# Splitting the K and V loads over two issuing queues, and moving half of the output projection forward, in a grouped-query attention kernel that reads a cache

## The chip, the cores and the metric

The kernel runs on one core of a Trainium2 chip. The metric is the device time of one execution in microseconds (us). Each execution has a state: fast, slow (over 1.5% above the fastest of the same kernel), or unknown when a kernel ran only once.

Engines: PE is the tensor engine (PEld is its weight load, which overlaps the matmuls), ACT is ScalarE, DVE is VectorE, POOL is GpSimd, SP is SyncE. "SPq" and "ACTq" are the DMA-issuing instructions of SyncE and ScalarE. A "unit" is one batch with one pair of key/value heads; there are 32, and each needs one K load and one V load of 1 MB.

## The reference, cut to what matters

```python
# B, Sq, D = 8, 4, 512;  Hq, Hkv, Sk, Dh = 32, 8, 2048, 128;  bfloat16
q = (x @ wq) split into 32 heads of 128
k, v = k_cache, v_cache repeated for the 4 query heads of each kv head
scores = einsum("bhqd,bhkd->bhqk", q, k) * Dh ** -0.5
o = einsum("bhqk,bhkd->bhqd", softmax(scores), v)
return o.transpose(0, 2, 1, 3).reshape(B, Sq, Hq * Dh) @ wo
```

wq and wo are 4 MB each, the two caches 32 MB each: 72 MB are read for very little arithmetic.

## The kernel before: the parts that matter

All loads are issued by SyncE, one K and then one V, up to seven units ahead. Each unit is worked on in two halves ("steps"). The tensor engine transposes K, multiplies it with the queries, sums the denominators and multiplies the probabilities with V. ScalarE does the exponentials and one of the four copies of transposed K in each unit.

```python
def load(u):                                  # K, then V, on the sync queue
    ks[u] = kpool.tile([128, C, Dh], BF16, tag="k_sb", name="k_sb")
    nc.sync.dma_start(ks[u][:, :, :], k_cache[...])
    vs[u] = vpool.tile([128, C, Dh], BF16, tag="v_sb", name="v_sb")
    nc.sync.dma_start(vs[u][:, :, :], v_cache[...])
# ... (cut)
nc.sync.dma_start(wq_sb[:, :, :], wq...)
for u in range(PRE):                          # PRE = 7
    load(u)
# ... (cut: query projection)
for step in range(-2, NH):                    # NH = 64 half-units
    if step + 2 < NH:
        transpose_part(step + 2, 0)           # PE: 8 transposes (kp); then a copy (kt)
    if 0 <= step + 1 < NH:
        scores(step + 1)                      # PE: 16 matmuls (s_ps); ACT: 2 exponentials (probs)
    if step + 2 < NH:
        transpose_part(step + 2, 1)           # in odd half-units ACT makes the copy (kt)
    if step >= 0:
        values(step)                          # PE: denominators (l_ps), 16 matmuls with V (o_ps)
        if step % 2 == 1:
            u = step // 2 + PRE
            if u < NU:
                load(u)
            elif u == NU:
                for h0, n in WO_PIECES:       # six pieces of wo, after the last V
                    load_wo(h0, n)
for h in range(Hq):                           # whole projection at the end, 32 matmuls (out_ps)
    nc.tensor.matmul(out_ps, lhsT=oT_all[h], rhs=wo_sb[h], ...)
```

A landing semaphore is the counter that tells of a load's arrival. The traces show eight of them, given to the loads in turn. A load is issued only when the load that used its semaphore before has landed: K4 shares the one of K0, which landed at 16.10 us, and was issued at 16.11. When such a wait is next in an engine's instruction stream, the engine does nothing else until it ends (8.48 us of ScalarE, shown below).

The softmax here doesn't subtract the row's maximum and nothing guards it: scores larger than these inputs give would overflow.

## Time and profile before

| | before |
|---|---|
| time, median of 3 runs | 195.59 us (195.52 to 196.03) |
| span of the profiled run | 193.9 us |
| a K or V load lands every | 2.48 us (unit: 4.97 us) |
| last K, last V, last wo piece land | 175.7, 178.2, 189.6 us |
| attention ends (last o_ps matmul) | 183.7 us |
| projection ends | 190.8 us |

These are lines of the page of the profile of the kernel before. In the first four, the span is cut in 40 equal slices; a digit is the busy share, or the granted clock, in tenths, and GB/s is what the DMA engines moved. The next two are the chain of work that ended last, by engine and by line. The last is a group of instructions: count, busy time, mean ns of one, then the idle time before them and what ended it.

```profile
PE   1019698887788868988877878598887878877893
PEclk9999789999999996999999999889999999996999
DMA  6989999999999999999999999999999999999960
GB/s 223 433 382 429 414 419 428 411 422 419 411 429 407 416 424 416 421 419 414 422 416 419 421 414 422 421 416 421 417 414 419 414 421 426 411 394 320 328 208 7
...
DMA 88%; PE 7%; SPq 2%; ACT 1%; issue 0%; DVE 0%; ACTq 0%
DMA k_sb<-in_k_cache_dram 88%; PE out_ps L223 4%; PE kp L134 2%; SPq L79 1%; SPq L84 1%; PE s_ps L150 1%; ACT kt L137 1%; PE l_ps L169 0%; PE o_ps L189 0%; DVE out_sb L230 0%; ACTq L257 0%; SPq L70 0%; SPq L69 0%; ACT probs L156 0%; ACTq L156 0%
...
L134 PE MATMUL kp<-ident,k_sb 128*128 128x128 bf16 x1024 | 83.2, 228 | 29.2 <-DMA k_sb<-in_k_cache_dram 29.0
```

The DMA engines are full from about 5 us to the end, and the chain consists of K loads. In the middle the tensor engine is eight tenths busy. Its one large wait, 29.0 us, is for K; the transposes of a unit start 0.05 us after its K lands, in nearly every unit.

### The profile page before, as it was taken

What the parts mean: (1) busy time and instruction counts of PE and PEld (TensorE: products, weight loads), DVE (VectorE), ACT (ScalarE), POOL (GpSimd) and SP (SyncE); (2) the same over time, 40 slices, a digit from 0 to 9 for tenths busy, and PEclk for the clock granted to TensorE, in tenths of its full rate; (3) what the DMA queues carried; (4) which work ended last, traced back from release to release, by engine and by line L of the source; (5) the groups of instructions that cost most, each with busy time, mean ns of one, the idle gap of its engine ahead of it and who ended that gap; (6) DMA issues with size and microseconds to landing.
All of it is one profiled execution on the core that took longest, in us unless ns stands there. A gap on an engine that the chain in (4) does not pass through costs nothing.

```text
span 193.9 us, 7655 instructions
## 1 busy us (share of the span) xinstructions
PE 146.2 (75%) x3492; PEld 137.8 (71%) x3492; DVE 95.4 (49%) x201; ACT 83.5 (43%) x165; POOL 0.7 (0%) x6
## 2 busy tenths in 40 slices
PE   1019698887788868988877878598887878877893
PEld 0019598777787768987777777498877777777741
DVE  4002366556555554665566665265555556663401
ACT  2003455444445551654444544355455555551500
POOL 1000000000000000000000000000000000000000
PEclk9999789999999996999999999889999999996999
DMA  6989999999999999999999999999999999999960
GB/s 223 433 382 429 414 419 428 411 422 419 411 429 407 416 424 416 421 419 414 422 416 419 421 414 422 421 416 421 417 414 419 414 421 426 411 394 320 328 208 7
DMA packets 13680, 76.05 MB, mean 392 GB/s; under 512 B 1168, under 2 KB 5328, under 8 KB 5328
## 3 DMA queue, kind: packets, MB, share of 16 engines
q1 hardware_dynamic: 13648, 75.57, 95.7%
q8 instruction: 27, 0.44, 0.9%
q14 instruction: 5, 0.04, 0.1%
HBM read 75.53 MB, written 0.03 MB: 390 GB/s over the span
## 4 chain that ended last, share of the span: by engine, by line
DMA 88%; PE 7%; SPq 2%; ACT 1%; issue 0%; DVE 0%; ACTq 0%
DMA k_sb<-in_k_cache_dram 88%; PE out_ps L223 4%; PE kp L134 2%; SPq L79 1%; SPq L84 1%; PE s_ps L150 1%; ACT kt L137 1%; PE l_ps L169 0%; PE o_ps L189 0%; DVE out_sb L230 0%; ACTq L257 0%; SPq L70 0%; SPq L69 0%; ACT probs L156 0%; ACTq L156 0%
## 5 line engine op out<-in xcount | busy, mean ns | idle before, releaser
L134 PE MATMUL kp<-ident,k_sb 128*128 128x128 bf16 x1024 | 83.2, 228 | 29.2 <-DMA k_sb<-in_k_cache_dram 29.0
L139 DVE COPY kt<-kp 128x1024 bf16<-128x1024 bf16 x96 | 66.0, 691 | 61.8 <-PE kp L134 50.8
L134 PEld LDWEIGHTS <-k_sb 128*128 128x128 bf16 x1024 | 62.6, 102 | 32.2 <-DMA k_sb<-in_k_cache_dram 31.9
L156 ACT ACTIVATE probs<-s_ps 64x256 bf16<-64x256 f32 x128 | 48.3, 378 | 83.7 <-PE s_ps L150 82.1
L150 PE MATMUL s_ps<-qT_all,kt 128*128 128x32 bf16 x1024 | 37.1, 177 | 1.0 <-ACT kt L137 0.5
L189 PE MATMUL o_ps<-probs,v_sb 128*128 128x32 bf16 x1024 | 36.1, 177 | 0.5 <-issue 0.5
L150 PEld LDWEIGHTS <-kt 128*128 128x128 bf16 x1024 | 33.4, 97 | 1.6 <-DVE kt L139 0.7
L189 PEld LDWEIGHTS <-v_sb 128*128 128x128 bf16 x1024 | 32.9, 97 | 0.6 <-issue 0.6
L137 ACT COPY kt<-kp 128x1024 bf16<-128x1024 bf16 x32 | 32.4, 1012 | 0.8
L169 PE MATMUL l_ps<-probs,ones 128*128 128x128 bf16 x256 | 20.0, 219 | 0.7 <-issue 0.4
L177 DVE TENSOR_REDUCE l_sb<-l_ps 128x32 f32<-128x128 f32 x32 | 9.3, 291 | 21.9 <-PE l_ps L169 21.9
L169 PEld LDWEIGHTS <-ones 128*128 128x128 bf16 x256 | 15.7, 98 | 1.1 <-issue 1.1
L184 DVE RECIPROCAL r_sb<-l_sb 128x32 f32<-128x32 f32 x32 | 11.3, 353 | 1.1
L114 PE MATMUL psq<-xT_sb,wq_sb 128*128 128x32 bf16 x128 | 3.6, 188 | 10.5 <-DMA wq_sb<-in_wq_dram 10.5
L114 PEld LDWEIGHTS <-wq_sb 128*128 128x128 bf16 x128 | 3.5, 104 | 10.6 <-DMA wq_sb<-in_wq_dram 10.6
L197 DVE TENSOR_TENSOR oT_all<-o_ps,r_sb 128x32 bf16<-128x32 f32 x32 | 6.1, 192 | 3.6 <-PE o_ps L189 0.4
L121 ACT ACTIVATE qT_all<-psq 128x256 bf16<-128x256 f32 x4 | 1.5, 385 | 14.2 <-PE psq L114 14.2
L223 PE MATMUL out_ps<-wo_sb,oT_all 128*32 128x512 bf16 x32 | 7.1, 379 | 0.0
L223 PEld LDWEIGHTS <-oT_all 128*32 128x32 bf16 x32 | 3.1, 97 | 3.6
L230 DVE CAST out_sb<-out_ps 32x512 bf16<-32x512 f32 x1 | 0.7, 679 | 6.5 <-PE out_ps L223 6.5
L105 PE MATMUL xtp<-ident,x_sb 32*128 32x32 bf16 x4 | 0.5, 190 | 2.7 <-DMA x_sb<-in_x_dram 2.5
L105 PEld LDWEIGHTS <-x_sb 32*128 32x128 bf16 x4 | 0.3, 113 | 2.8 <-DMA x_sb<-in_x_dram 2.5
(10 smaller groups left out, 4.3 us busy)
## 6 DMA issues: line engine op xcount, KB each, us to landing
k_sb<-in_k_cache_dram SPq DMA_DIRECT2D x32, 1024.0 KB, 19.9
v_sb<-in_v_cache_dram SPq DMA_DIRECT2D x32, 1024.0 KB, 19.9
wq_sb<-in_wq_dram SPq DMA_DIRECT2D x1, 4096.0 KB, 12.5
wo_sb<-in_wo_dram SPq DMA_DIRECT2D x3, 1024.0 KB, 21.7
wo_sb<-in_wo_dram SPq DMA_DIRECT2D x1, 512.0 KB, 10.1
wo_sb<-in_wo_dram SPq DMA_DIRECT2D x2, 256.0 KB, 7.6
x_sb<-in_x_dram SPq DMA_DIRECT2D x1, 32.0 KB, 1.7
out_dram<-out_sb SPq DMA_DIRECT2D x1, 32.0 KB, 1.5
```

The lines of the kernel that those rows point to most:

```text
L114: nc.tensor.matmul(psq[:, h, :], lhsT=wq_sb[:, r, hh * 128 : (hh + 1) * 128], rhs=xT_sb[:, r, :], start=(r == 0), stop=(r == R - 1),)
L134: nc.tensor.transpose(kp[:, c, :], ks[u][:, c0 + c, :], ident[:, :])
L137: nc.scalar.copy(out=k_t[:, :, :], in_=kp[:, :, :])
L139: nc.vector.tensor_copy(out=k_t[:, :, :], in_=kp[:, :, :])
L150: nc.tensor.matmul(s_ps[:, c, :], lhsT=k_t[:, c % (HC // 2), :], rhs=q2, start=True, stop=True)
L156: nc.scalar.activation(out=pr[rows, hf * HC : (hf + 1) * HC, cols], in_=s_ps[rows, :, cols], func=EXP)
L169: nc.tensor.matmul(l_ps[:, :, :], lhsT=ones[:, :], rhs=pr[:, c * 4 : (c + 1) * 4, :], start=(c == 0), stop=(c == C // 4 - 1),)
L177: nc.vector.tensor_reduce(out=l_sb[:, :], in_=l_ps[:, :, :].rearrange("d c q -> d q c"), axis=mybir.AxisListType.X, op=mybir.AluOpType.add,)
L184: nc.vector.reciprocal(r_sb[:, :], l_sb[:, :])
L189: nc.tensor.matmul(o_ps[u][:, :], lhsT=vs[u][:, cc, :], rhs=pr[:, cc, :], start=(cc == 0), stop=(cc == C - 1),)
L197: nc.vector.tensor_tensor(out=oT_all[:, p * HP : (p + 1) * HP, b, :], in0=o_ps[u][:, :].rearrange("d (h s) -> d h s", h=HP), in1=r_sb[:, : ...
L223: nc.tensor.matmul(out_ps[:, :], lhsT=oT_all[:, h, :, :].rearrange("d b s -> d (b s)"), rhs=wo_sb[:, h, :], start=(h == 0), stop=(h == Hq ...
```

## The change

The intent: K goes on the sync queue and V on the scalar queue, so that two engines share the issuing. K runs about three units ahead of V, since it is needed first. The first half of wo is loaded in the middle, and the two quarters of the projection that it allows are done early in the next head pair (in units 9 and 17), so that only 16 of the 32 projection matmuls are left for the end. The other half of wo comes last, on the scalar queue.

```diff
-    def load(u):
+    def load_k(u):
         ks[u] = kpool.tile([128, C, Dh], BF16, tag="k_sb", name="k_sb")
         nc.sync.dma_start(...)
+    def load_v(u):
         vs[u] = vpool.tile([128, C, Dh], BF16, tag="v_sb", name="v_sb")
-        nc.sync.dma_start(...)
+        nc.scalar.dma_start(...)
 ... (cut: vpool has 5 buffers instead of 7; out_ps has a PSUM pool of its own, psum_o one buffer)
-    nc.sync.dma_start(wq_sb[:, :, :], ...)
-    for u in range(PRE):
-        load(u)
+    nc.scalar.dma_start(wq_sb[:, :, :], ...)
+    for u in range(4):
+        load_k(u)
+    for u in range(3):
+        load_v(u)
+    for u in range(4, KB):                  # KB = 7, VB = 5
+        load_k(u)
 ... (cut: at the end of values(step); u, hf = divmod(step, 2); p, b = units[u])
+        if hf == 0:
+            if u >= 1:
+                load_v(u - 1 + VB)
+            else:
+                for v in range(3, VB):
+                    load_v(v)
+            if b == 1 and p in (1, 2):
+                project(p - 1)              # 8 matmuls
+        else:
+            load_k(u + 1 + KB if u else KB)
+            if u == 0:
+                load_k(KB + 1)
+            if b == 3 and p < 2:
+                load_wo(nc.sync, p * HP, HP)
+            if u == NU - 1:
+                project(2)
+                project(3)
+            if u + VB == NU:
+                for h0, n in ((16, 8), (24, 4), (28, 2), (30, 2)):
+                    load_wo(nc.scalar, h0, n)
```

No byte, matmul or exponential is added or taken away.

## The prediction, made before the changed kernel ran

> **What bounds the kernel now.** The DMA. The chain of waits puts 88% of the span on K loads; the slices show 411 to 430 GB/s from 5 to 165 us. A K or V load (1 MB) lands every 2.48 us, so a unit (one batch, one head pair) costs 5.0 us of DMA; the tensor engine needs about 4.0 us a unit where it waits for nothing (timeline, 26.4 to 30.4 us). The built program takes eight landing semaphores in turn, so each DMA waits for the landing of the one eight before: issue to landing is 19.9 us, eight loads.
> Tail: the last K lands at 175.7, the last V at 178.2; the last unit's work lasts until 183.7 (8.0 us, part at granted clock 0.5); the projection, 32 matmuls of 0.22 us, runs to 190.8 without a wait; the span ends at 193.9. The last wo piece lands at 189.6: DMA and tensor engine end about 1 us apart.
>
> **What the change moves.** No byte or matmul goes away. ScalarE now issues V and half of wo; both queues share the eight semaphores. The Trainium skill ("DMA: Bandwidth & Descriptors", "Issuing engines are not separate DMA queues") says that both queues run on the same 16 engines and interleave; this trace has one queue and can't show it. I expect the same rate.
> - Start: two queues issue side by side, about -0.4 us (one issue). wq shares bandwidth with K, so the first projection starts after 13.7 us; off the critical path, because loads stay queued.
> - Projection: 16 of 32 matmuls move into idle time of the middle: -3.5 us in the tail.
> - wo: half, about 5.7 of the 11.4 us after the last V, moves to the middle. All loads still end near 189, so the last V lands later, near 183.5.
> - K ahead: the last K lands with V of unit 28, near 176. The three last V then come every 2.5 us, but the tensor engine needs 4.0 us a unit. It has 8 value steps, 6 score steps, 5 half-unit transposes and 4 denominators left: about 12.6 us at full clock, then 3.5 us of projection: 192.1 against 190.8 before. The tail is then bound by the tensor engine: the gain is lost.
> - ScalarE blocks: issues of wo behind queued descriptors took 11.97, 4.30, 2.71, 1.33 and 1.17 us, against 0.33 for K or V. On SyncE this cost nothing; now four wo issues stand in ScalarE's order before the exponentials of half-unit 57. ScalarE is held 4 to 8 us, and the tensor engine waits 2 to 5 us for probabilities.
>
> Sum: -0.4 +1.3 +2 (a moderate stall): about 198.5 us.
>
> **What would show it.** DMA slices near 418 GB/s in the middle; long wo issues in ScalarE's queue; an idle tensor engine before values or denominators, released by ScalarE, near 178 to 182; out_ps x16 at the end; V of units 29 to 31 landed well before use; a chain ending on tensor engine and ScalarE with well over today's 8%.
>
> **What would make it wrong.** If a second queue hides the cost per descriptor (1 KB ones take 46 ns, 22 GB/s an engine; 8 KB ones 312 ns, 26), loads end 1 to 4 us earlier and the kernel gains. If the scalar queue takes the wo issues without blocking: 195 to 197. If ScalarE's waits for landings hold the tensor engine so long that the loads run dry in the middle: over 203.
>
> Chances: faster by over 2% 0.06, within 2% 0.52, slower by over 2% 0.42; range 194.0 to 202.5.

## More of the kernel before

The waits of the tensor engine before (engine, line, tile, what it waited for; us in total, times, longest):

```profile
PE kp L134 <- DMA k_sb<-in_k_cache_dram: 29.0, 28, 2.4
...
PE o_ps L189 <- issue: 0.5, 1, 0.5
...
PE kp L134 <- issue: 0.2, 1, 0.2
```

"issue" is a wait for nothing that the profile shows. Here there is hardly any of it.

## The result, and the profile after

The changed kernel took 203.62 us (median of 4 runs, 202.95 to 204.91). The ratio is 1.041 (95% interval 1.035 to 1.047): 4.1% slower. A ratio is the mean time of one kernel's fast runs over the mean of the other's fast runs of the same rounds, so it is not quite the ratio of the medians quoted. The profiled run was a fast one; its span is 201.2 us.

The same lines of the page, of the changed kernel:

```profile
PE   1006970699969784999769976999777887777983
PEclk9999998599978998599999999999999999999999
DMA  7989999999999999999999999999999999998100
GB/s 241 456 381 427 417 423 419 422 419 419 420 420 411 403 404 412 420 420 419 419 416 404 403 412 417 417 415 417 422 422 415 414 422 422 414 344 300 61 3 7
...
DMA 47%; PE 40%; issue 5%; ACT 4%; ACTq 2%; DVE 0%; SPq 0%
DMA wo_sb<-in_wo_dram 27%; DMA k_sb<-in_k_cache_dram 20%; PE kp L146 16%; PE s_ps L162 8%; PE o_ps L201 6%; PE out_ps L220 4%; PE l_ps L181 4%; ACT kt L149 2%; ACTq L96 2%; ACT probs L168 1%; PE psq L126 1%; ACT L133 1%; DVE out_sb L261 0%; ACTq L288 0%; ACT qT_all L133 0%
...
L146 PE MATMUL kp<-ident,k_sb 128*128 128x128 bf16 x1024 | 81.6, 226 | 1.6 <-issue 1.6
```

The loads did not suffer. They fill the DMA engines as before, and the last piece of wo lands at 189.9 us against 189.6. But some eleven microseconds follow in which nothing is loaded (the last three slices: 61, 3 and 7 GB/s) and the tensor engine still works. The chain has changed from loads to work: PE 40% where it was 7%. The wait of the transposes for K, 29.0 us before, is gone. Others stand in its place. The waits of the tensor engine after:

```profile
PE s_ps L162 <- ACT kt L149: 10.9, 5, 7.5
PE o_ps L201 <- issue: 7.6, 7, 1.7
PE s_ps L162 <- issue: 7.4, 8, 1.4
PE out_ps L220 <- DMA wo_sb<-in_wo_dram: 3.8, 2, 1.9
...
PE kp L146 <- issue: 1.6, 1, 1.6
```

Two of these are waits for ScalarE's copies and for wo, which the change makes possible. The others are "issue" waits: 17.7 us in all (with 1.1 us of l_ps), against about 1 us before.

Where the lag arises is told by when each unit's last multiplication with V ended, taken from the records of the two traces (us from the start of the span):

| unit | before | after | later by |
|---|---|---|---|
| 1 | 31.4 | 41.7 | 10.3 |
| 5 | 51.1 | 60.7 | 9.6 |
| 9 | 71.0 | 86.5 | 15.5 |
| 13 | 92.4 | 106.4 | 14.0 |
| 21 | 133.8 | 145.8 | 12.0 |
| 27 | 163.4 | 177.0 | 13.6 |
| 31 | 183.7 | 194.5 | 10.8 |

The kernel is 8 to 16 us late from the second unit to the last and never gets this back. At the end, 16 fewer projection matmuls give back 3.5 us: 10.8 - 3.5 = 7.3 us, which is the difference of the two spans. The timeline of the changed kernel shows the first hold and what happened near the end (start, duration, engine, what; in brackets the idle time before it and what ended it):

```profile
29.19 0.68 DVE L151 COPY kt<-kp 128x1024 bf16<-128x1024 bf16 x1
32.06 2.81 ACTq L90 DMA_DIRECT2D v_sb<-in_v_cache_dram  x2
34.97 0.78 ACT L168 ACTIVATE probs<-s_ps 64x256 bf16<-64x256 f32 x2 [8.48 <-DMA k_sb<-in_k_cache_dram]
35.77 1.01 ACT L149 COPY kt<-kp 128x1024 bf16<-128x1024 bf16 x1
...
36.84 0.39 PE L162 MATMUL s_ps<-qT_all,kt 128*128 128x32 bf16 x8 [7.53 <-ACT kt L149]
...
176.60 5.00 ACTq L96 DMA_DIRECT2D wo_sb<-in_wo_dram  x3
...
180.54 0.48 PE L162 MATMUL s_ps<-qT_all,kt 128*128 128x32 bf16 x13 [1.17 <-issue]
...
181.70 1.58 ACT L168 ACTIVATE probs<-s_ps 64x256 bf16<-64x256 f32 x4 [4.12 <-PE kp L146]
182.53 0.38 PE L181 MATMUL l_ps<-probs,ones 128*128 128x128 bf16 x4 [0.84 <-ACT probs L168]
```

At the start, ScalarE's stream has the issues of V3 and V4 ahead of the exponentials. V3 could be issued only at 32.06, just after K3 had landed (32.03), and V4 at 34.53, just after K4 (34.51). ScalarE sat still for 8.48 us, and the tensor engine for 7.53 us. The granted clock was 0.5 from 34.2 to 41.0 us, so the tensor engine's first work after the hold went slowly too. Near the end, four wo issues held ScalarE from 176.2 to 181.6 us, as predicted in kind, but the tensor engine lost only 0.84 us to it beyond one "issue" stop.

In the middle the first half of wo is late. The first piece was issued on SyncE at 53.1 us and landed at 79.9, 26.7 us later, while V9 to V11, issued after it on the other queue, landed before it. The first projection stands at a fixed place in the tensor engine's stream and waited 1.85 us for it; then its 8 matmuls took 3.57 us at a granted clock of 0.5, about as long as 16 take at the end. The second piece took 27.6 us, with the same wait again. The K loads behind these pieces on SyncE's queue came late too (K12 at 84.9). Around 100 us ScalarE was held once more: V16 was issued at 100.77, right after K16 landed at 100.75.

From unit 22 on there is no such hold before the one near 176 us, and V lies in SBUF 7 to 10 us before it is used. Yet the kernel catches up with nothing: units 22 to 27 took 5.2 us each, (177.0 - 145.8) / 6.

### The profile page after: what moved, and what is told of

Its sections match the earlier page's. It is cut to its first block, busy times and chain, and to the rows that moved or that the text cites. A ratio compares the mean times of both kernels' runs of the same rounds, so it can differ in the third digit from the quotient of the medians.

```text
span 201.2 us, 7664 instructions
## 1 busy us (share of the span) xinstructions
PE 148.2 (74%) x3492; PEld 137.9 (69%) x3492; DVE 93.6 (47%) x201; ACT 83.4 (41%) x165; POOL 0.7 (0%) x6
## 4 chain that ended last, share of the span: by engine, by line
DMA 47%; PE 40%; issue 5%; ACT 4%; ACTq 2%; DVE 0%; SPq 0%
DMA wo_sb<-in_wo_dram 27%; DMA k_sb<-in_k_cache_dram 20%; PE kp L146 16%; PE s_ps L162 8%; PE o_ps L201 6%; PE out_ps L220 4%; PE l_ps L181 4%; ACT kt L149 2%; ACTq L96 2%; ACT probs L168 1%; PE psq L126 1%; ACT L133 1%; DVE out_sb L261 0%; ACTq L288 0%; ACT qT_all L133 0%
## 5 line engine op out<-in xcount | busy, mean ns | idle before, releaser
L146 PE MATMUL kp<-ident,k_sb 128*128 128x128 bf16 x1024 | 81.6, 226 | 1.6 <-issue 1.6
L146 PEld LDWEIGHTS <-k_sb 128*128 128x128 bf16 x1024 | 61.8, 100 | 3.0 <-issue 3.0
L162 PE MATMUL s_ps<-qT_all,kt 128*128 128x32 bf16 x1024 | 40.7, 178 | 18.8 <-ACT kt L149 10.9
L162 PEld LDWEIGHTS <-kt 128*128 128x128 bf16 x1024 | 34.8, 97 | 21.6 <-ACT kt L149 11.4
L201 PE MATMUL o_ps<-probs,v_sb 128*128 128x32 bf16 x1024 | 36.7, 177 | 7.6 <-issue 7.6
L181 PE MATMUL l_ps<-probs,ones 128*128 128x128 bf16 x256 | 20.8, 224 | 2.2 <-ACT probs L168 1.1
L181 PEld LDWEIGHTS <-ones 128*128 128x128 bf16 x256 | 16.5, 101 | 2.6 <-issue 2.6
L220 PE MATMUL out_ps<-wo_sb,oT_all 128*32 128x512 bf16 x32 | 9.1, 441 | 3.8 <-DMA wo_sb<-in_wo_dram 3.8
```

What stands on the lines that cost most here:

```text
L146: nc.tensor.transpose(kp[:, c, :], ks[u][:, c0 + c, :], ident[:, :])
L162: nc.tensor.matmul(s_ps[:, c, :], lhsT=k_t[:, c % (HC // 2), :], rhs=q2, start=True, stop=True)
L181: nc.tensor.matmul(l_ps[:, :, :], lhsT=ones[:, :], rhs=pr[:, c * 4 : (c + 1) * 4, :], start=(c == 0), stop=(c == C // 4 - 1),)
L201: nc.tensor.matmul(o_ps[u][:, :], lhsT=vs[u][:, cc, :], rhs=pr[:, cc, :], start=(cc == 0), stop=(cc == C - 1),)
L220: nc.tensor.matmul(out_ps[:, :], lhsT=oT_all[:, h, :, :].rearrange("d b s -> d (b s)"), rhs=wo_sb[:, h, :], start=(h == 0), stop=(h == Hq ...
```

## The experiments

The questions: which part of the change costs the time, and why is nothing caught up? My first theory was that the waits in ScalarE's stream (the holds) are the cause. Rivals: the early wo and projection, the order of K and V, or two rings sharing the DMA engines (a ring is the queue in which the descriptors, the pieces of a load, of one issuing engine stand). The "issue" stops raised a further one later: the tensor engine itself is slower while loads run. Times are medians; ratios are to the kernel before, in the same rounds. All results are correct except the three marked wrong.

| experiment | us | ratio [95%] | attention ends |
|---|---|---|---|
| before | 195.59 | 1 | 183.7 |
| after | 203.62 | 1.041 [1.035, 1.047] | 194.5 |
| e4 before, V from ScalarE | 208.23 | 1.065 [1.063, 1.066] | 196.2 |
| e13 before, V from GpSimd | 201.79 | 1.030 [1.029, 1.032] | 189.4 |
| e1 after, all loads on SyncE | 200.44 (one of 4 runs slow) | 1.022 [1.018, 1.027] | (slow run) |
| e7 before, early wo and projection | 197.48 | 1.011 [1.006, 1.016] | 189.6 |
| e8 before, K ahead as in after | 196.53 | 1.004 [1.002, 1.006] | 184.9 |
| e2 after, projection at the end | 207.41 | 1.060 [1.058, 1.062] | 196.2 |
| e6 after, early projections later | 205.89 | 1.052 [1.049, 1.055] | 196.3 |
| e3 after, last wo from SyncE | 206.04 | 1.052 [1.051, 1.054] | 197.5 |
| e5 after, first V from SyncE | 204.49 | 1.045 [1.043, 1.047] | 195.6 |
| e9 after, V from GpSimd | 206.23 | 1.054 [1.048, 1.059] | 197.7 |
| e14 after, fewer PE instructions | 203.99 | 1.042 [1.041, 1.044] | 194.4 |
| b1 before, K one unit ahead | 195.35 | 0.999 [0.998, 1.000] | 181.3 |
| b2 b1, fewer PE instructions | 195.70 | 1.001 [0.998, 1.003] | 179.8 |

Every expectation is quoted. Several missed both of the ranges that they named (e3, e4, e6, e8, e9 and e13).

### e4: only the second queue

The kernel before, with V issued by ScalarE and nothing else changed.

```diff
-        nc.sync.dma_start(vs[u][:, :, :], ...)
+        nc.scalar.dma_start(vs[u][:, :, :], ...)
```

> The kernel before with one edit: V is issued by ScalarE. Order of loads, wo last and the projection at the end stay. Theory Q: each V issue waits in ScalarE's order for the landing of the load eight before it, which is the V of about three units later than the one in work, so exponentials are held and the tensor engine trails the loads by some units; it cannot catch up in the tail: 199 to 206 us. Theory O: 194 to 197 us.

It took 208.23 us, 6.5% more: more than the whole change. The timeline of e4 shows the largest hold, in unit 5:

```profile
64.42 0.34 ACTq L84 DMA_DIRECT2D v_sb<-in_v_cache_dram  x1
64.86 1.58 ACT L156 ACTIVATE probs<-s_ps 64x256 bf16<-64x256 f32 x4 [10.13 <-issue]
65.69 0.58 PE L169 MATMUL l_ps<-probs,ones 128*128 128x128 bf16 x4 [6.95 <-ACT probs L156]
```

ScalarE stood for 10.13 us until a V load was issued, with four exponentials behind it, and the tensor engine waited 6.95 us for the probabilities. From unit 5 (15.6 us late) to the end (12.5 us late) little is made up, although V lay landed for 16 to 24 us from there on. Part of the lateness is older than this hold: V0 landed at 5.96 us, before K0, which came at 23.14 instead of 16.10, and unit 1 already ended 10.2 us late. So the second queue alone does harm, and a delay stays.

### e13: the second queue without ScalarE

V is issued by GpSimd, which has next to no other work, so no exponential can wait behind a load.

```diff
-        nc.sync.dma_start(vs[u][:, :, :], ...)
+        nc.gpsimd.dma_start(vs[u][:, :, :], ...)
```

> The kernel before with V issued by GpSimd instead of SyncE: the same split as in e4 (208.2 us), but by an engine that has nothing else to do. If ScalarE's waits for landings in its own order are what e4 lost by: 194.5 to 197.5 us. If two rings are bad as such: 203 to 209 us.

It took 201.79 us, 3.0% more. There is no hold by ScalarE, and still there is a loss: the two rings lose the order of the loads. V runs ahead (V17 lands at 104.1 and is used 10 us later), at K's expense (K17 lands at 107.7, and at 103.2 before), and K is what the tensor engine waits for by name, beside "issue" stops. From the waits of e13:

```profile
PE kp L134 <- DMA k_sb<-in_k_cache_dram: 13.1, 14, 2.5
...
PE o_ps L189 <- issue: 7.0, 6, 1.5
```

Most of the loss is there at the start. The first transposes come at 20.3 us instead of 17.1, since V loads share the bandwidth with wq and K0; unit 1 ends 4.3 us later than before, and the whole attention 5.7. GpSimd also makes the identity matrix after its first issues, but it was ready before K0 landed at 20.27. So of e4's 6.5%, a loss of about 3.0 comes with a second queue even without ScalarE. I put the other 3.5 down to ScalarE's holds, but this is not shown: e4's first transposes came at 23.2 us, 2.9 later than e13's, and the trace lists GpSimd's queue as another kind ("software_dynamic", SyncE's and ScalarE's are "hardware_dynamic"), which may cost or save something of its own.

### e1: the change on one queue

The changed kernel with all loads on SyncE: K ahead, early wo and early projection remain.

```diff
-        nc.scalar.dma_start(vs[u][:, :, :], ...)
+        nc.sync.dma_start(vs[u][:, :, :], ...)
-    nc.scalar.dma_start(wq_sb[:, :, :], ...)
+    nc.sync.dma_start(wq_sb[:, :, :], ...)
-                    load_wo(nc.scalar, h0, n)
+                    load_wo(nc.sync, h0, n)
```

> The changed kernel with every load back on SyncE's queue, in the same program order (K ahead of V, half of wo early, half last, projection as in the change). Theory Q (the split costs: ScalarE is held by its loads' waits for landings, wo is overtaken by V in the second ring, so the tensor engine falls behind): 196 to 199 us, no idle tensor engine of 7 us near 30 us, wo pieces of the middle landing within 22 us of their issue (26.7 and 27.6 in the changed kernel). Theory O (K ahead of V by itself makes the tail too long, the queues do not matter): 202 to 205 us. What is between says how much is whose.

The fast runs are 2.2% slower than before. (Its profiled run was slow, so no reading rests on its trace.) About half of the 4.1% therefore goes with the second queue, and half is in the rest of the change.

### e7 and e8: the rest of the change, one part at a time

e7 is the kernel before, one queue, K and V in the old order, with two pieces of wo early and half of the projection early. e8 is one queue with K ahead of V as in the changed kernel, and wo and projection last.

```diff
 # e7, against before
+                if b == 3 and p < 2:
+                    load_wo(p * HP, HP)
+                if b == 1 and p in (1, 2):      # at the even step, half a unit earlier
+                    project(p - 1)
 # e8, against after: every load on nc.sync (V, wq, wo), and
-            if b == 1 and p in (1, 2):
-                project(p - 1)
-            if b == 3 and p < 2:
-                load_wo(nc.sync, p * HP, HP)
+            (all six pieces of wo after the last V, all four project() at the end)
```

> The kernel before with the early half of wo and of the projection alone: one queue, K and V in the old alternation. The loads end at the same time, so the last K lands some 5.5 us later than 175.7 us, the last unit's 7 to 8 us follow, and then 3.6 us of projection instead of 7.1: 196.5 to 198.5 us. If the shorter projection at the end were a gain by itself: 192 to 194 us.

> K ahead of V alone: one queue (SyncE), buffers 7 and 5, wo and the whole projection last. V of units 29 to 31 then land 2.5 us apart, faster than the tensor engine can take them (about 4.0 us a unit and up to 1.5 us of instruction fetch on top). Theory O (the order makes the tail long): attention ends near 186 instead of 183.7 us, total 197 to 200 us. If the order is harmless: 194 to 196 us.

e7 took 1.1% more and e8 0.4% more. Neither part pays alone. In e8 the tensor engine waits for V instead of K, and the loads still set the pace:

```profile
PE o_ps L201 <- DMA v_sb<-in_v_cache_dram: 25.0, 24, 4.5
```

In e7 the early wo pushes K and V later (last K at 181.7, before 175.7), and attention ends at 189.6. Added, these two make 1.5%, against 2.2% measured together in e1; the second queue takes it from there to 4.1%.

### e2 and e6: is the early projection the trouble?

e2 takes the early projection out of the changed kernel; the loads stay where they are. e6 does the two early quarters four units later, when wo has long landed.

```diff
 # e2
-            if b == 1 and p in (1, 2):
-                project(p - 1)
             if u == NU - 1:
-                project(2)
-                project(3)
+                for pp in range(G2):
+                    project(pp)
 # e6
-            if b == 1 and p in (1, 2):
+            if b == 5 and p in (1, 2):
```

> The changed kernel with all 32 projection matmuls at the end; loads and queues as in the change. If the tensor engine is the limit from about 50 us to the end, the two waits for wo in the middle (1.8 and 1.9 us in the profile, plus half clock at the first) and their 16 matmuls are taken out of its way and 3.6 us come back at the end: 198 to 201 us. If the loads set the end and the early projection ran in idle time (as predicted): 206 to 208 us.

> The changed kernel with the projections of head-pair groups 0 and 1 four units later (batch 5 instead of 1), when their wo has landed. If the tensor engine is the limit from about 50 us on, the waits for wo (1.8 and 1.9 us) and what they drag along are gained: 198 to 201.5 us. If they were made up for later by idle time: 203 to 204 us.

Both are slower than the changed kernel, and e6 missed both of its ranges. e2 lacks what the early projection was to bring: its 32 matmuls at the end take 7.08 us, where the 16 left in the changed kernel take 3.63 (a gain of 3.45; predicted: 3.5). In both the wait for wo is gone, and unit 9 ends at 79.9 and 79.4 instead of 86.5 us. Then the next hold takes the place: ScalarE cannot issue V16 before K16 lands at about 101.1, and unit 13 ends at 108.4 and 110.0 (106.4 after). Taking one hold away gains nothing when a later one is tied to the same stream of loads. The early projection pays at the end what was expected of it; the time goes elsewhere.

### e5: the hold at the start taken away

V of the first five units comes from SyncE.

```diff
-        nc.scalar.dma_start(vs[u][:, :, :], ...)
+        (nc.sync if u < VB else nc.scalar).dma_start(vs[u][:, :, :], ...)
```

> The changed kernel with V of the first five units issued by SyncE, so that ScalarE is not held at the start (in the changed kernel the tensor engine stands still for 7.5 us near 30 us, while ScalarE waits to issue V 3 and V 4 for the landing of K 3 and K 4). If lost time of the tensor engine anywhere is lost at the end: 196 to 199 us. If a later hold (V 16 waits for the landing of K 16 at 101 us, behind wo) sets the tensor engine's place again, it changes nothing: 202 to 205 us.

Unit 1 ends at 35.4 us, 6.4 us earlier than in the changed kernel. Already by unit 3 that is gone (50.6 against 49.6): V3, now on SyncE's queue, landed at 46.96, and the tensor engine waited 5.3 us for it. Later V16 waits for K16 again (issue 99.88, landing 99.86), and unit 13 ends at 107.3 against 106.4. The total is 1.045, where the changed kernel had 1.041.

### e3: the wo issues off ScalarE

The last half of wo is issued by SyncE, so that the 5.4 us in ScalarE near the end fall away.

```diff
-                    load_wo(nc.scalar, h0, n)
+                    load_wo(nc.sync, h0, n)
```

> The changed kernel with only the last half of wo moved from ScalarE's to SyncE's queue. In the changed kernel's profile ScalarE is held from 176.6 to 181.6 us by three of these issues. If that hold costs what the prediction said (2 to 5 us of waiting tensor engine): 198.5 to 201.5 us. If the tensor engine was behind anyway and stood still only for the 1.2 + 0.8 us seen near 180 and 182: 201.5 to 203.5 us.

It took 206.04 us, slower still. The hold by wo is gone, but in this program V28 has another wait in front of it: it was issued at 165.06, right after K28 landed at 165.04. ScalarE stood 6.29 us, and unit 25 took 10.05 us. Which semaphore a load gets follows from the order of all loads of both queues, so moving four issues changed the waits of others. This run does not measure what I wanted, the cost of the wo issues alone; it shows that the holds cannot be moved singly.

### e9: the changed kernel with V from GpSimd

ScalarE issues wq only; V comes from GpSimd and the last wo from SyncE.

```diff
-        nc.scalar.dma_start(vs[u][:, :, :], ...)
+        nc.gpsimd.dma_start(vs[u][:, :, :], ...)
-                    load_wo(nc.scalar, h0, n)
+                    load_wo(nc.sync, h0, n)
```

> The changed kernel with V issued by GpSimd (idle otherwise) and the last half of wo by SyncE: two queues still, but ScalarE issues only wq and waits for no landing in the loop. If ScalarE's in-order waits for landings are what the split costs: 197 to 201 us, as with one queue (200.4), and no idle tensor engine of several us in the middle. If the second ring itself costs (wo overtaken by V, later instruction fetches): 202 to 206 us.

The theory that ScalarE's holds are the cause, and nothing else, falls here: 206.23 us, no faster than the changed kernel. The waits of the tensor engine of e9 show another hold:

```profile
PE out_ps L220 <- DMA wo_sb<-in_wo_dram: 12.3, 1, 12.3
PE kp L146 <- DMA k_sb<-in_k_cache_dram: 9.4, 10, 1.7
PE o_ps L201 <- issue: 7.7, 6, 1.5
```

Up to unit 8 the tensor engine keeps in step with K. Then the first projection waits 12.3 us for wo, whose first piece needed 40.3 us from issue to landing. Unit 9 takes 21.7 us and ends at 90.5 (71.0 before), 19.5 us late; unit 27 is still 17.9 us late, and the end 14. A hold of another kind has the same effect, and again little is caught up. What all these kernels have in common is that the tensor engine does not catch up.

### e10, e11 and e12: how fast is the tensor engine without waits?

These three give wrong results. e10 loads K and V of four units only and uses them again and again, so that no loads run after about 45 us. e11 adds loads that nobody reads, two of 0.75 MB a unit, on SyncE's queue. e12 issues one of the two from ScalarE instead. No computation reads the added data.

```diff
 # e10, against before
-    PRE = 7
+    PRE = 4
     def load(u):
+        if u >= PRE:
+            ks[u], vs[u] = ks[u - PRE], vs[u - PRE]
+            beside(u)                       # e10: nothing
+            return
 # e11: what beside(u) does
+        for eng, cache in ((nc.sync, k_cache), (nc.sync, v_cache)):
+            d_sb = dump.tile([128, 24, Dh], BF16, tag="d_sb", name="d_sb")
+            eng.dma_start(d_sb[:, :, :], cache[...][:, :24, :])
 # e12, against e11
-        for eng, cache in ((nc.sync, k_cache), (nc.sync, v_cache)):
+        for eng, cache in ((nc.sync, k_cache), (nc.scalar, v_cache)):
```

> Wrong result on purpose: K and V of four units are reused, no load at all from about 32 us until wo at the end. Measures the tensor engine's own pace. If the stops of 1.2 to 1.5 us after each 16 KB instruction fetch come from the loads' traffic, they shrink below 0.5 us and a unit takes 3.9 to 4.1 us; if they are the fetch's own, a unit takes 5.0 to 5.3 us as in the changed kernel.

> As the quiet kernel, with two loads of 0.75 MB a unit on SyncE's queue into buffers that nobody reads (wrong result on purpose). Tensor engine waits for no load. Stops after instruction fetches of 0.5 to 1.1 us, as with all loads on one queue; 4.4 to 4.9 us a unit.

> As the one-ring kernel, with the two idle loads of a unit on SyncE's and on ScalarE's queue. If two rings delay the instruction fetch more than one: stops of 1.2 to 1.5 us, 4.9 to 5.3 us a unit. If the number of rings is of no matter: as with one ring.

They took 165.72, 187.62 and 187.22 us (one run each, state unknown, so I lean on what differs by tens of per cent). The windows view gives a stretch: its length, the busy time and instructions of each engine, the granted clock, the DMA share and GB/s. e10, e11 and e12 in this order:

```profile
60.00:120.00 60.00, 59.37 (x1541) 57.77 (x1539) 41.72 (x90) 37.24 (x74) 0.00 (x0) 1.00 0.01 4
```

```profile
60.00:140.00 80.00, 65.01 (x1664) 62.75 (x1664) 45.24 (x96) 40.36 (x81) 0.00 (x0) 1.00 1.02 414
```

```profile
60.00:140.00 80.00, 68.61 (x1767) 66.30 (x1765) 47.87 (x102) 42.63 (x86) 0.00 (x0) 1.00 0.96 362
```

Without loads the tensor engine is busy 59.37 of 60 us, and a unit takes 4.05 us (units 8 to 25). Beside loads of 414 GB/s, of which it needs nothing, it is busy 65.01 of 80 us at the same granted clock, and a unit takes 5.04 us (expected: 4.4 to 4.9). With two queues a unit takes 4.76 us, but the loads ran at 362 GB/s, 13% slower, so this does not compare the rings at equal traffic. Later in e12, from 149 to 163 us, when wo's small descriptors were queued beside the other ring, the stops grew to 1.7 to 2.0 us and units 26 to 28 took 6.0 us each (in e11, with wo on the one ring, the stops were 1.4 to 1.6 us then). So a second ring is not needed for the stops, but the rival that it lengthens them stays open. The difference between e10 and e11 is in the stops called "issue". The waits of the tensor engine in e11:

```profile
PE kp L148 <- issue: 7.6, 6, 1.6
PE s_ps L164 <- issue: 6.9, 6, 1.4
PE o_ps L203 <- issue: 5.4, 5, 1.2
```

And this is the timeline of one of them in e11, in the middle of eight transposes that had all they needed:

```profile
83.64 0.33 PE L148 MATMUL kp<-ident,k_sb 128*128 128x128 bf16 x3
84.86 0.44 PE L148 MATMUL kp<-ident,k_sb 128*128 128x128 bf16 x5 [0.89 <-issue]
```

I counted the tensor engine's matmuls and weight loads in the trace. In the steady part of e11 these stops come before numbers 1217, 1473, 1729, 1985, 2241 and so on: every 256 instructions, without exception from 1217 to 5825. A unit has 208 of them. Shortly before each stop a DMA packet of 16 KB is in the records (27 such packets, 0.44 MB, "q8 instruction" on the page). From the start of this packet to the tensor engine going on it takes 2.3 to 2.6 us. The Trainium skill ("Runtime: NRT & Kernel Launch", "Instruction fetch mechanics") describes just such blocks: 16 KiB, 256 instructions, fetched by DMA. It calls the cost of crossing a block boundary "mostly hidden". In e10 that holds: no stop over 0.3 us between 60 and 120 us. Beside saturated loads it does not: each stop is 0.9 to 1.6 us. The packet itself comes late there. In e10 (60 to 120 us) it begins 4.2 to 5.0 us before the tensor engine reaches the next block, in e11 only 0.6 to 1.4 us. e11 also has its own control: its last load lands at 154.7 us, the last stop ends at 153.3, and units 27 to 30 take 4.0 us each:

```profile
156.00:172.00 16.00, 15.89 (x419) 15.49 (x416) 11.16 (x24) 9.99 (x21) 0.00 (x0) 1.00 0.01 3
```

In the changed kernel the stops fall on the same instruction numbers (1473, 1985, 2241, 3009, 3777, 4801 to 6337).

The stops cost about 1.1 us x 208/256, or 0.9 us a unit, and 4.05 + 0.9 is 4.95 us. Or, counted otherwise: in e11 a block of 256 instructions takes 6.15 us from one stop's end to the next (60.35 to 134.15, twelve blocks), so 208 take 5.0 us. The loads deliver a unit in 4.97 us. Here is why so little is caught up: while loads run at full rate, the tensor engine has hardly any speed to spare. In the kernel before, the packets come at the same spacing (6.2 us), but its tensor engine waited for K some 0.96 us in nearly every unit. So it reached each new block 1.9 us or more after the packet's start, and its weight loads stood there for over 0.3 us only four times (0.6 at most). As I read it, the waits for K hid the stops.

### e14: fewer instructions for the tensor engine

If the fetch sets the pace, fewer instructions should help. The denominators are summed in 2 matmuls of 512 columns instead of 8 of 128: 12 fewer of about 208 instructions a unit.

```diff
-            l_ps = psum_l.tile([128, 4, NQ], FP32, tag="l", name="l_ps")
-            for c in range(C // 4):
+            l_ps = psum_l.tile([128, 16, NQ], FP32, tag="l", name="l_ps")
+            for c in range(C // 16):
```

> The changed kernel with the denominators in 2 matmuls of 512 columns a unit instead of 8 of 128: the same columns and the same matmul time, 12 of about 208 tensor-engine instructions a unit fewer. If instruction fetch sets the tensor engine's pace while loads are queued, a unit costs about 0.29 us less of it (6.2 us a block of 256): 198 to 201.5 us. If it does not: 203 to 204.5 us.

I expected 198 to 201.5 us and measured 203.99: a miss. The tensor engine was faster between the holds (unit 7 ends at 68.5, not 70.8; units 19 to 24 take 4.5 us each, not 5.0) and then stood longer at the holds. The waits of the tensor engine in e14:

```profile
PE s_ps L162 <- ACT kt L149: 13.0, 8, 7.9
...
PE out_ps L220 <- DMA wo_sb<-in_wo_dram: 7.8, 2, 6.8
PE l_ps L181 <- ACT probs L168: 4.7, 4, 3.9
...
PE o_ps L201 <- issue: 3.3, 4, 1.1
```

Against the changed kernel the "issue" waits shrank and the waits for wo and ScalarE grew by as much; attention ends at 194.4 instead of 194.5. As I read it, the place in time is set by the holds, which are tied to landings of the loads, and the stops only prevent a recovery between them. The last hold (3.9 us, up to 182 us) is so late that what was gained before it does not show in the end.

### b1 and b2: a better kernel?

From what was learned, the simplest gain: one queue, the old order, with K one unit ahead of V, so that after the last V less is left to do. b2 adds e14's denominators.

```diff
 # b1, against before
-    for u in range(PRE):
-        load(u)
+    load_k(0)
+    for u in range(PRE - 1):
+        load_k(u + 1)
+        load_v(u)
 # in the loop: load_k(u + 1), load_v(u) instead of load(u)
```

> The kernel before with one edit: K one unit ahead of V in SyncE's queue. K of the last unit lands about 2.5 us earlier (173.2 us), V last as before (178.2). Attention ends near 181 to 182 instead of 183.7 us, and the projection then runs into the landing of the last wo piece at 189.6: 194.5 to 195.5 us, 0.2 to 0.6% faster.

> K one unit ahead and the denominators in 2 matmuls a unit. The loads set the pace in the middle, so the fewer instructions gain only in the tail, where wo's landing is the next limit: 194 to 195.5 us; not slower than K one ahead alone by more than 0.2%.

b1 took 195.35 us: 0.13% less than before (0.01 to 0.25%), so much the same. Attention ends 2.4 us earlier, at 181.3. But the last wo piece still lands at 189.6, the projection needs it, and the loads are the bound again. b2 took 195.70 us, just outside its range and not different from before, although its attention ends at 179.8.

## Why the prediction was right or wrong, point by point

The prediction was 198.5 us, in a range from 194.0 to 202.5, with "within 2%" the likeliest. It was 203.62, outside the range.

**Right.** The rate and the end of the loads did not change ("I expect the same rate"; last landing 189.9 against 189.6 us). The Trainium skill's statement that the prediction used ("DMA: Bandwidth & Descriptors", "Issuing engines are not separate DMA queues") agrees with this. The last V landed at 182.8 (predicted "near 183.5"). The projection's part at the end took 3.63 us instead of e2's 7.08, a gain of 3.45 (predicted 3.5). ScalarE was held 5.4 us by the wo issues (predicted 4 to 8). The chain ends on the tensor engine, at 40% where it had 7.

**Wrong: the tensor engine's pace.** The step that failed is "the tensor engine needs about 4.0 us a unit where it waits for nothing (timeline, 26.4 to 30.4 us)". It was one unit, read in a stretch in which no stop fell. Beside full loads a unit takes 5.0 us (e11), and 5.2 in the changed kernel between units 21 and 27. The loads deliver one in 4.97 us, so the reserve of 1 us a unit on which the sum rested was not there.

**Wrong, because of it: "off the critical path, because loads stay queued".** With 1 us of reserve a unit, ten units would have made up the 10 us lost at the start. In fact a delay at 20 to 40 us is still there at 184. The loads were indeed always queued; the work behind them was late.

**Left out: the holds before the tail.** The sum had ScalarE held only by wo. It was held by the landing semaphores of K at 29 to 35 us (the tensor engine stood 7.5 us) and near 100 us. The first projection then waited for wo, which took 26.7 us to land. "If ScalarE's waits for landings hold the tensor engine so long that the loads run dry in the middle: over 203" came near to it, but with the wrong condition: it went over 203 without the loads ever running dry.

**Wrong: "the last K lands with V of unit 28, near 176".** K31 landed at 180.7, V28 at 169.5. K stood behind the slow wo pieces on SyncE's queue, so the lead of three units was lost in landing order.

**Too large: the tail.** Of "the tensor engine waits 2 to 5 us for probabilities", about 0.84 us came on top of an "issue" stop. The tensor engine was already so late that it was still busy with transposes and scores during most of ScalarE's hold.

**What stays open.** How the 10.8 us divide between the holds is not settled: whenever one was removed (e2, e3, e5, e6, e9) another took its place. I found no way to take all of them away in the two-queue kernel, since the framework assigns the semaphores. That the stops are instruction fetches rests on their place at every 256th instruction, on the 16 KB packets just before them, on e10 against e11 and on the end of e11; no run changed the fetch itself without changing the work. Whether a second ring makes the stops longer at equal traffic is open too. Why an issue behind queued small descriptors blocks the issuing engine was not tested.

## What to carry to other kernels

When an engine looks idle for a fifth of the time beside saturated loads, do not count that idle time as reserve: measure its pace with the same loads running and nothing to wait for, as e11 did, before you rely on it to absorb a delay. Do not put loads that may have to wait for a landing into the stream of an engine on which the others depend. Be wary of a load with small descriptors that must arrive at a given time beside a second ring of large ones (wo took 26.7 and 40.3 us here; not isolated). When one hold is taken away and the time does not move, look for the next one that is tied to the same event.

## What the Trainium skill lacked or had wrong

- "Runtime: NRT & Kernel Launch", "Instruction fetch mechanics" says that crossing a 16 KiB boundary is "mostly hidden". Runs e10 and e11 show that this depends on the load traffic: no stop over 0.3 us from 60 to 120 us without loads, a stop of 0.9 to 1.6 us at every 256th instruction of the tensor engine beside loads of 414 GB/s. Here that is 0.9 us of every 5 us.
- "DMA: Bandwidth & Descriptors", "Queues, rings and completion order" says that each DMA engine round-robins between queues at packet granularity. It does not draw the consequence for loads with descriptors of different size, which the runs fit: wq (32 KB descriptors) beside K0 (8 KB) moved its 4 MB by 15.2 us while 1 MB of K0 needed until 16.4; wo (1 KB descriptors) beside V (8 KB) took 26.7 us to land after and 40.3 us in e9, while on one queue, in e7, it took 21.5. I have not isolated it in a run of its own.
- "Perfetto Trace Analysis", "DMA Instruction — HWDGE (DVE, Sync)" has the issuing engine busy until all descriptors of a DMA are generated. I found no page that says how long this can last when many small descriptors are queued. Issues of wo took 11.97, 4.30 and 2.71 us on SyncE in the kernel before, and 2.52 us on ScalarE after, and two K issues behind wo 8.22 and 9.44 us, where the issue of a K or V load mostly takes 0.33 us.
- "DMA: Bandwidth & Descriptors", "Issuing engines are not separate DMA queues" says that issuing from several engines only saves issue time. It does not say that it can also cost: e13, with nothing changed but V on GpSimd's queue, was 3.0% slower. As I read it, this is because the two queues lose the order in which K and V are needed (V17 landed at 104.1 us, K17 at 107.7; before, K17 came first, at 103.2).
